# Attention of two transformer layers: part of the softmax exponentials given to VectorE, and TensorE's order set by a list schedule

## The chip, the cores and the metric

One core of one Trainium2 chip. The time is the device time of one execution in microseconds (us), the median over several executions. A kernel's profile is one execution with every instruction recorded. In its lines PE is TensorE, PEld its weight loads, DVE VectorE, ACT ScalarE, POOL GpSimd.

## The reference, cut to what matters

```
x = x + attention(layernorm(x))      # S=2048, D=640, 32 heads of 20
x = x + mixer(layernorm(x))          # 2048 -> 1536 -> 2048 over the tokens, gelu
(both once more, same weights)

scores = einsum("bhqd,bhkd->bhqk", q, k) * 20 ** -0.5
p = softmax(scores)                  # 32 x 2048 x 2048 exponentials a layer
o = einsum("bhqk,bhkd->bhqd", p, v)
```

A head has 20 values, padded to 32. The kernel works in *units* of 4 heads x 128 keys x 512 queries: 512 units, or 2048 single-head pieces ("heads" below, each 128x512), a layer. A *group* is the 16 units that share 4 heads and 512 queries; there are 32 groups a layer.

## The kernel before

Scores come from 64-row matmuls with half of the query rows masked, two at a time, and are repeated where TensorE has nothing else to do. One ScalarE instruction takes three heads:

```python
def s_matmul(St, slot, n, j):
    qb, g, kt = units[n]; jj = j // 2
    q = qm_tiles[(qb, g)][j % 2]                      # masked copy of Q
    pe(nc.tensor.matmul(St[:, slot, :], lhsT=KT[64 * jj:64 * jj + 64, g, kt * 128:(kt + 1) * 128],
                        rhs=q[64 * jj:64 * jj + 64, :], start=True, stop=True, tile_position=(64 * jj, 0)))
def emit_exp(t):
    nc.scalar.activation(out=P[:, 0:ncs, :]..., in_=St[:, 0:ncs, :]..., func=ACT.Exp, scale=SCALE)
# loop over tiles: scores of t+1 (repeated if no side work is at hand), exp of t,
# products P x V of older units, then a budget of side work (projections, output product,
# a partial mixer product per query block)
```

Each row block is layer-normed twice before the mixer. The products of a group add up in one PSUM tile `acc`, which VectorE transposes and normalizes.

The softmax here doesn't subtract the row's maximum and nothing guards it: scores larger than these inputs give would overflow.

## Time and profile before

| | us |
|---|---|
| time, median of 12 runs (2116.21 to 2120.33) | 2117.78 |
| span of the profiled run | 2114.6 |
| attention 1, first to last exponential | 923.8 |
| attention 2 | 924.2 |
| all else | 266.7 |

The attention rows are the distance from the start of the first exponential to the end of the last in the timeline (48.9 to 972.7 and 1098.2 to 2022.3).

### The profile page before, as it was taken

How to read it: one execution, taken by the hardware profiler on the slowest of the kernel's cores; microseconds unless marked ns; L12 is line 12 of the kernel's file. 1: busy time of each engine (PE TensorE's matmuls, PEld its weight loads, DVE VectorE, ACT ScalarE, POOL GpSimd, SP SyncE). 2: the span in 40 equal slices, each digit the busy share in tenths (PEclk: the TensorE clock that was granted, in tenths of full speed). 3: DMA queues.
4: the chain of work that ended last, by engine and by line, in shares of the span. 5: the costliest groups of instructions: out<-in, count | busy, mean ns of one | idle time of the engine just before them, and what ended most of it. 6: DMA issues, size and time to landing. Idle time of an engine off the chain costs nothing.

```text
span 2114.6 us, 31885 instructions
## 1 busy us (share of the span) xinstructions
PE 1924.5 (91%) x13100; PEld 655.4 (31%) x13278; DVE 623.9 (30%) x1391; ACT 1934.8 (91%) x1508; POOL 166.8 (8%) x250
## 2 busy tenths in 40 slices
PE   7999999999999999896999999999999999999969
PEld 4222222233223323222542222222332233232235
DVE  6122233212422042223542122332123221422252
ACT  5999999999999999995449999999999999999952
POOL 2000000110012001100000000001000110111000
PEclk9999999999999999998999999999999999999989
DMA  5000000110034012223620000101100430232145
GB/s 129 1 1 1 1 20 19 61 53 10 29 63 65 1 38 43 37 42 94 213 81 1 1 1 1 35 25 61 45 26 26 75 53 1 57 50 39 33 120 181
DMA packets 90739, 96.89 MB, mean 46 GB/s; under 512 B 9696, under 2 KB 68192, under 8 KB 90592
## 3 DMA queue, kind: packets, MB, share of 16 engines
q1 hardware_dynamic: 70464, 71.22, 10.9%
q0 software_dynamic: 20128, 23.62, 7.6%
q8 instruction: 104, 1.70, 0.4%
q14 instruction: 43, 0.35, 0.1%
HBM read 55.48 MB, written 39.32 MB: 45 GB/s over the span
## 4 chain that ended last, share of the span: by engine, by line
ACT 58%; PE 24%; issue 13%; DVE 4%; DMA 1%; POOL 1%; SPq 0%; another core or an unknown queue 0%; POOLq 0%; ACTq 0%; DVEq 0%
ACT P L345 57%; PE S L317 10%; PE y L746 4%; PE acc L551 3%; PE misc L223 3%; PE pp L214 1%; DMA ua<-uacc 1%; PE misc L453 1%; DVE bnst L158 1%; POOL rstd L165 1%; DVE bnst L159 0%; DVE utmp L685 0%; PE pp L223 0%; DVE T L354 0%; DMA x0in<-in_A_x_dram 0%
## 5 line engine op out<-in xcount | busy, mean ns | idle before, releaser
L345 ACT ACTIVATE P<-S 128x1536 bf16<-128x1536 f32 (+1 forms) x1366 | 1839.7, 1502 | 9.7 <-PE S L317 9.0
L317 PE MATMUL S<-qev,KT 64*128 64x512 bf16 x2962 | 836.2, 377 | 102.1 <-ACT P L345 95.5
L317 PE MATMUL S<-qod,KT 64*128 64x512 bf16 x3052 | 837.9, 379 | 20.8 <-ACT P L345 3.7
L317 PEld LDWEIGHTS <-KT 64*128 64x128 bf16 x6014 | 326.3, 93 | 657.1 <-issue 487.8
L551 PE MATMUL acc<-P,Vaug 128*32 128x512 bf16 x4096 | 409.9, 389 | 6.2 <-DVE T L354 4.3
L551 PEld LDWEIGHTS <-Vaug 128*32 128x32 bf16 x4096 | 106.5, 92 | 439.0 <-issue 439.0
L432 DVE COPY ustg<-misc 128x512 f32<-128x512 f32 (+1 forms) x144 | 70.1, 487 | 291.8 <-PE misc L426 261.1
L165 POOL TENSOR_TENSOR rstd<-veps,mhalf 128x1 f32<-128x1 f32 x96 | 54.0, 563 | 1194.3 <-DVE veps L163 1167.3
L437 POOL DMA_DIRECT2D uacc<-ustg x96 | 83.0, 864 | 464.8 <-DVE ustg L432 434.9
L746 PE MATMUL y<-uT,w2s 128*128 128x128 bf16 (+1 forms) x754 | 106.7, 297 | 4.2 <-ACT uT L689 2.7
L426 PE MATMUL misc<-h2st,w1st 128*128 128x128 bf16 (+1 forms) x524 | 105.0, 295 | 5.0 <-issue 2.9
L513 DVE CAST QTq<-misc 128x512 bf16<-128x512 f32 x62 | 42.9, 691 | 205.5 <-PE misc L223 205.5
L513 DVE CAST KT<-misc 128x512 bf16<-128x512 f32 x56 | 38.7, 691 | 212.0 <-PE misc L223 207.7
L354 DVE STREAM_TRANSPOSE T<-acc 128x512 f32<-128x512 f32 x64 | 45.9, 717 | 182.8 <-PE acc L551 182.8
L223 PE MATMUL misc<-hh,wq_pad 128*128 128x512 bf16 x272 | 91.0, 386 | 0.1
L276 DVE TENSOR_SCALAR qev<-QTq,mask_ev 128x512 bf16<-128x512 bf16 x64 | 22.5, 352 | 228.7 <-PE S L317 228.2
L223 PE MATMUL misc<-hh,wk_pad 128*128 128x512 bf16 x254 | 82.1, 385 | 1.5 <-issue 1.3
L746 PEld LDWEIGHTS <-w2s 128*128 128x128 bf16 x768 | 59.6, 98 | 50.0 <-issue 5.3
L453 PE MATMUL misc<-wo_pad,attnT 128*128 128x128 bf16 (+1 forms) x361 | 71.8, 298 | 0.6 <-issue 0.6
L76 ACT CAST Vaug<-pp 128x500 bf16<-128x500 f32 (+1 forms) x32 | 14.3, 454 | 50.5 <-PE pp L214 50.5
L426 PEld LDWEIGHTS <-w1st 128*128 128x128 bf16 x576 | 33.9, 97 | 61.1 <-issue 58.8
L462 DVE TENSOR_TENSOR x1s<-misc,xin 128x512 f32<-128x512 f32 (+1 forms) x48 | 23.5, 490 | 98.1 <-PE misc L453 98.1
(81 smaller groups left out, 788.7 us busy)
## 6 DMA issues: line engine op xcount, KB each, us to landing
uacc<-ustg POOLq DMA_DIRECT2D x72, 256.0 KB, 4.0
w2s<-in_B_w_dram SPq DMA_DIRECT2D x16, 768.0 KB
w1st<-in_B_w_dram SPq DMA_DIRECT2D x36, 256.0 KB
xd<-x1s SPq DMA_DIRECT2D x24, 320.0 KB
x1in<-xd SPq DMA_DIRECT2D x24, 320.0 KB
ua<-uacc SPq DMA_DIRECT2D x24, 320.0 KB
xd<-x2s SPq DMA_DIRECT2D x16, 320.0 KB
xin<-xd SPq DMA_DIRECT2D x16, 320.0 KB
```

Source lines behind the costliest of these rows:

```text
L165: nc.gpsimd.tensor_tensor(out=rstd[:], in0=veps[:], in1=mhalf[:], op=ALU.pow)
L223: pe(nc.tensor.matmul(t[:, :], lhsT=wpad[:, dt_, g, :], rhs=st.hT[:, dt_, tb * 512:(tb + 1) * 512], start=(dt_ == 0), stop=(dt_ == NDT - 1)))
L317: pe(nc.tensor.matmul(St[:, slot, :], lhsT=KT[64 * jj:64 * jj + 64, g, kt * 128:(kt + 1) * 128], rhs=q[64 * jj:64 * jj + 64, :], start=Tru ...
L345: nc.scalar.activation(out=P[:, 0:ncs, :].rearrange("p a b -> p (a b)"), in_=St[:, 0:ncs, :].rearrange("p a b -> p (a b)"), func=ACT.Exp, ...
L354: nc.vector.transpose(out=T1[:], in_=acc[:])
L426: pe(nc.tensor.matmul(t[:, 0:w], lhsT=states[fp]["w"][:, sti, ftl * 128:(ftl + 1) * 128], rhs=tiles4[sti][:, c0:c1], start=(sti == 0), sto ...
L432: nc.vector.tensor_copy(out=stg[:, 0:w], in_=t[:, 0:w])
L437: nc.gpsimd.dma_start(out=dst, in_=stg[:, 0:w], accum_op=ALU.add)
L453: pe(nc.tensor.matmul(t[:, 0:w], lhsT=attnT[:, g, ttl * 128:(ttl + 1) * 128], rhs=wo_pad[:, g, c0:c1], start=(g == 0), stop=(g == NG - 1)))
L513: nc.vector.tensor_copy(out=dst_ap, in_=t[:, :])
L551: pe(nc.tensor.matmul(acc[32 * j:32 * j + 32, :], lhsT=Vaug[:, (kt * H + hh) * VW:(kt * H + hh) * VW + 32], rhs=P[:, ci % 3, :], start=(kt ...
L746: pe(nc.tensor.matmul(y[:, 0:w], lhsT=w2s[:, ft, sl * 128:(sl + 1) * 128], rhs=uT[:, ft, c0:c1], start=(ft == 0), stop=(ft == NF - 1)))
```

## The change

Its intent: ScalarE's exponentials are the wall and VectorE is mostly idle, so VectorE takes some units. It turns a score into the bits of a bfloat16 power of two: J makes a fixed-point exponent in uint16, TT shifts and offsets it twice, and the sum of the two piecewise-linear results is close to a true exponential. Softmax divides by the sum of the weights, so a common factor doesn't matter. Core of the diff, with cuts marked by `...`:

```diff
-    R_DEFAULT=1, FILL_NOPV=3.0, ...
+SHIFTS = (0.0, 0.4927)
+NP_BUFS = 4; NJ_BUFS = 2; NT_BUFS = 5; ...
+# planned durations: PE_MM = 216.0, LAT_PE = 230.0, LAT_ACT = 240.0, LAT_V = 120.0 ...
-    lhsT=KT[64 * jj:64 * jj + 64, ...], rhs=q[64 * jj:64 * jj + 64, :]   # masked Q
+    lhsT=KT[32 * j:32 * j + 32, ...], rhs=get_QT(st, qb, g)[32 * j:32 * j + 32, :]
+            SLOT_N = (3, 2)                      # heads per ScalarE tile, in turn
+            def do_J(start):                     # one head, PSUM f32 -> uint16
+                nc.vector.tensor_scalar(out=d["jt"][:, j * 512:(j + 1) * 512], in0=Dt[:],
+                    scalar1=SCALE * LOG2E * 256.0, scalar2=127.0 * 256.0, op0=ALU.mult, op1=ALU.add)
+            def do_T(start):                     # four heads, one of two terms
+                nc.vector.tensor_scalar(out=tt_[:], in0=jt[:], scalar1=0.5, scalar2=TERM_C[i], ...)
+                ... tt_[...].bitcast(BF16)       # goes into the products like P
+            def warm(gap):                       # planned TensorE gap -> matmuls of zero weights
+                k = int(gap // PE_MM)
+                ...
+            # choice on TensorE: ScalarE's scores, VectorE's scores, products, side work
+            urgent = ("need" in f and is_urgent(f["need"])) or (gi >= NGR - 3 and not f.get("need"))
-            # in words: two layer norms per row block; partial mixer product per query block, added up by DMA
+            # in words: one layer norm (on GpSimd); one partial mixer product near the end, 12 row blocks deep
-                nc.vector.tensor_tensor(out=T2[:], ...)   # normalization
+                nc.gpsimd.tensor_tensor(out=T2[:], ...)
```

The kernel gives out PSUM in banks of 128x512 float32, eight in all: 3 + 2 for ScalarE's two tiles, one for VectorE's scores (SD), one for `acc`, one for side work.

## The prediction

> **What bounds the kernel now.** I read the page's busy shares and 40 slices first, then the chain that ended last.
>
> ```profile
> PE 1924.5 (91%) x13100; PEld 655.4 (31%) x13278; DVE 623.9 (30%) x1391; ACT 1934.8 (91%) x1508; POOL 166.8 (8%) x250
> ...
> ACT  5999999999999999995449999999999999999952
> ...
> ACT P L345 57%; PE S L317 10%; PE y L746 4%; PE acc L551 3%; PE misc L223 3%; PE pp L214 1%; DMA ua<-uacc 1%; PE misc L453 1%; DVE bnst L158 1%; POOL rstd L165 1%; DVE bnst L159 0%; DVE utmp L685 0%; PE pp L223 0%; DVE T L354 0%; DMA x0in<-
> ```
>
> Two engines look full, but there are two plateaus of ACT at 9 with a dip between (the first mixer) and a drop at the end (the second), and the exponential holds the chain. Next, the costliest groups tell which of the two is really full.
>
> ```profile
> L345 ACT ACTIVATE P<-S 128x1536 bf16<-128x1536 f32 (+1 forms) x1366 | 1839.7, 1502 | 9.7 <-PE S L317 9.0
> L317 PE MATMUL S<-qev,KT 64*128 64x512 bf16 x2962 | 836.2, 377 | 102.1 <-ACT P L345 95.5
> L317 PE MATMUL S<-qod,KT 64*128 64x512 bf16 x3052 | 837.9, 379 | 20.8 <-ACT P L345 3.7
> ```
>
> ScalarE lost only 9.7 us ahead of 1839.7 us of exponentials, while TensorE waits for ScalarE. There are 6014 score matmuls in the records where two layers need 2 x 2048 = 4096: a third are the deliberate repeats of the code, so TensorE's 91% is padded. ScalarE is the wall and VectorE, at 30%, is the engine with room. Then I cut the span by stage (start; attention 1; mixer 1; attention 2; mixer 2).
>
> ```profile
> core 0: us, PE busy (x) PEld busy (x) DVE busy (x) ACT busy (x) POOL busy (x), PEclk, DMA share, GB/s
> 0.00:46.60 46.60, 33.42 (x258) 20.51 (x263) 34.40 (x120) 25.82 (x49) 12.71 (x26) 1.00 0.62 139
> 46.60:966.50 919.90, 852.86 (x5767) 265.45 (x5842) 236.16 (x486) 914.28 (x681) 67.69 (x96) 1.00 0.13 28
> 966.50:1096.50 130.00, 109.17 (x790) 62.07 (x802) 74.95 (x205) 47.85 (x63) 13.71 (x24) 0.92 0.49 156
> 1096.50:2016.00 919.50, 852.11 (x5762) 265.14 (x5837) 236.12 (x486) 914.22 (x680) 67.71 (x96) 1.00 0.14 31
> 2016.00:2114.60 98.60, 76.94 (x528) 42.24 (x537) 42.23 (x96) 32.58 (x39) 4.96 (x8) 0.91 0.53 161
> ```
>
> So each attention is 920 us, nearly all of it ScalarE, and the rest is 46.6 + 130.0 + 98.6 = 275 us.
>
> **What the Trainium skill says.**
> - "VectorE: DVE Perf Modes", section "The perf-mode tier table": a tensor_scalar between 16-bit SBUF tensors runs at four elements a cycle, 693 ns for 2048 elements; with a PSUM operand it falls to at most two, and to one for float32 (section "Why PSUM operands drop a tier"). The trace agrees in kind: 128x512 bf16 through tensor_scalar took 352 ns, under the 533 ns of one element a cycle at that page's 0.96 GHz; a cast of 128x512 from PSUM took 691 ns.
> - "TensorEngine Tiling (Array Packing)", section "Key Properties": a change of tiling mode drains TensorE. The trace agrees: matmuls of one mode start 0.21 us apart, but a value product that follows a score matmul starts 0.30 us after it, and a full-array one 0.34 us after the products. A switch costs about 0.1 us.
> - "TensorE: Matmul & The Clock Gate", section "Measured speedup vs the span model": four 32-row matmuls together gain 3.07 times. Not in this trace, which has two 64-row tiles; its four 32-column products do share 0.40 us.
> - "SBUF — State Buffer", section "SBUF: two separate sides": a VectorE instruction in a two-port mode and a GpSimd one exclude each other. No number for it in this trace.
>
> **The change part by part** (per layer, 512 units of 4 heads x 128 keys x 512 queries).
> 1. *It moves some units' exponential to VectorE.* Per unit: 4 instructions J, one head each, PSUM 128x512 to uint16, and 2 instructions TT on 2048 uint16, whose bits are read as bf16 and both multiplied into the accumulator. J is a 128x512 read of PSUM: 691 ns, less the overlap with its neighbour. Two VectorE instructions of 692 and 280 ns lasted 0.89 us together in the first tail, so the overlap is 82 ns; J costs 609 ns. TT: 693 (the skill's; no record before) less 82 is 611 ns. A unit is 4 x 609 + 2 x 611 = 3.66 us of VectorE.
> 2. *ScalarE's tiles become 3 and 2 heads in turn.* Before: 1839.7/1366 = 1347 ns for 3 heads. The record lasts 1503, so neighbours overlap by 156; the few 128x1024 records last 1089, hence 933 each. Five heads take 2280 ns, 456 a head, 1.82 us a unit (against 1.80).
> 3. *VectorE's other work.* 236 us per attention now. Out go the two query masks (32 x 0.70 = 22), the multiply of the normalization, now on GpSimd (32 x 0.69 = 22), the second layer norm (12 tiles: from about 3.9 to 1.2 us, 32) and two thirds of the partial sums' evictions (36 x 0.97 down to 12 x 0.97, 23). Left: 236 - 99 = 137 us.
> 4. *Ideal split.* With x units on VectorE: 1.82(512 - x) = 3.66x + 137, so x = 145 and both end at 668 us. That needs both engines without a gap.
> 5. *Why not ideal.* VectorE's scores have one PSUM bank. J (0.69), then a matmul and its latency (0.42 us from the start of a matmul to the eviction in the trace) make 1.14 us per head before any queueing at TensorE; with 0.2 for queueing and delays by other VectorE work, four heads take about 5.5 us, in whose gaps the two TT and the other work fit. x = 720/5.5 = 131. VectorE is then 131 x 3.66 + 137 = 616 us busy, and ScalarE 381 x 1.82 = 693 us; at about 96% occupied (the two-head tile leaves little time to refill the other bank set) this is 720 us.
> 6. *TensorE.* At 0.213 us: 610 score tiles, 130 us; say 60% of 524 single VectorE heads not hidden beside another, 67; products (381 + 2 x 131) x 4/4, 137, and a fifth more for incomplete quartets, 164; projections 59 x 5, 63; output projection and first mixer product, about 80. Sum 504 us. At 0.1 us a switch and about 4.5 switches per five heads (305 periods) come 137 us: 641 of 720, 89%. It fits, but barely; TensorE's repeats are gone.
> 7. *Tail.* One layer norm instead of two saves about 5 us after each attention; the GpSimd multiply and small instructions give back about 2. Net 3 each.
>
> Sum: 275 + 2 x 720 - 2 x 3 = 1709 us span. The time was 4.5 us above the span before (2119.1 against 2114.6), so **1714 us**.
>
> **The rivals.**
> - *TensorE takes over.* For: step 6 has 89% and a static order cannot refill a missed slot; a full-array filler of two matmuls plus a switch is 0.53 us, while the slack for the three-head tile is 933 less about 0.7 us. Against: the repeats were a third of the score matmuls and 4 row tiles overlap. It gives attentions near 775 us, 1825 us in all, and ScalarE would wait for S.
> - *TT is not at four elements a cycle* (unsigned integers, or the shared port). At two, TT is about 1.15 us, a unit 4.74 us; the ideal is 709, realistically 760, 1795 us in all. Against: dtype width and placement are what the page names.
> - *The single bank's loop is slower*, 6.3 us per unit: x = 118, ScalarE 717 us of work, about 745 us an attention, 1765 in all.
> - *The schedule is nearly perfect*, 680 us: 1635. For: the order comes from a list schedule whose durations (67 + 426.7 per head, 216, 600, 610) match the trace.
> - *The new tail costs more*: the last block's weights are loaded only after the partial mixer product ended. If that ends in the tail, some 10 us per layer are exposed. Its priority is raised in the last three groups, so I doubt it.
>
> **Range and chances.** Attention from 680 to 770 us gives 1634 to 1814; I take 1630 to 1810. The work moved is far larger than any of these terms: even the TensorE rival is 14% faster. Faster by over 2%: 0.97; within 2%: 0.015; slower: 0.015, for a throttled clock or a badly broken order.
>
> **What would show it.** Attention windows of 700 to 740 us with ScalarE 95 to 97% busy and about 1520 heads there per layer, VectorE 80 to 88%; J near 690 and TT near 690 ns; about 130 units a layer on VectorE (4 J and 2 TT each); a granted clock still 1.00 in attention. Wrong if ScalarE's idle ahead of its exponentials passes 8% with S as releaser (TensorE rival), if TT is over 1 us, or if VectorE's units are under 120. The start and the mixers should keep their 275 us within 10.

## More of the kernel before

The prediction shows the page's busy shares, chain and groups. One more line of the chain of waits, shares of the span by engine, is needed for comparison later:

```profile
ACT 58%; PE 24%; issue 13%; DVE 4%; DMA 1%; POOL 1%; SPq 0%; another core or an unknown queue 0%; POOLq 0%; ACTq 0%; DVEq 0%
```

ScalarE holds most of the chain; TensorE holds a quarter, and about half of that is its scores and products in attention (10% and 3% in the list by line, which the prediction shows).

## The result, and the profile after

| | before | after |
|---|---|---|
| time, median | 2117.78 (12 runs) | 1762.33 (8 runs, 1758.67 to 1770.1) |
| attention 1 / 2, first to last exponential | 923.8 / 924.2 | 748.5 / 754.1 |
| all else | 266.7 | 258.0 |
| heads a layer on ScalarE / VectorE | 2048 / 0 | 1556 / 492 |

The ratio is 0.8325 (95% interval 0.8311 to 0.8338). A ratio here is the mean time of one kernel's fast runs over that of the other's in the same rounds, so it isn't quite the ratio of the medians.

The page of the changed kernel, busy shares and the chain of waits by engine:

```profile
PE 1658.2 (94%) x12645; PEld 552.3 (31%) x12804; DVE 1341.2 (76%) x2348; ACT 1524.9 (87%) x1388; POOL 178.8 (10%) x298
...
PE 62%; DVE 17%; ACT 12%; issue 6%; DMA 1%; POOL 1%; SPq 0%; ACTq 0%; DVEq 0%; POOLq 0%
```

VectorE went from 30% to 76%. The chain has moved: 58% on ScalarE before, 62% on TensorE now. Shares of a chain are no proof where three engines wait on one another, but this is a first hint that TensorE has little slack left.

The groups of instructions, by shape (count, then busy us and mean ns, then idle time before them with its releasers):

```profile
L850 ACT ACTIVATE P<-S 128x1536 bf16<-128x1536 f32 x622 | 913.2, 1468 | 56.9 <-PE acc L479 38.9 <-PE S L351 9.1 <-PE SD L351 3.0
L802 DVE TENSOR_SCALAR J<-SD 128x512 uint16<-128x512 f32 x984 | 671.1, 682 | 254.2 <-PE SD L351 248.9 <-PE S L351 3.6
L850 ACT ACTIVATE P<-S 128x1024 bf16<-128x1024 f32 x622 | 648.6, 1043 | 17.1 <-PE acc L479 15.4 <-PE S L351 1.2
L823 DVE TENSOR_SCALAR TT<-J 128x2048 uint16<-128x2048 uint16 x492 | 343.3, 709 | 7.7
```

The 984 J are four per unit in two layers: 123 units a layer. ScalarE lost 74 us in all, VectorE waited 249 us for its scores from TensorE.

The span cut by stage (start, attention 1, mixer 1, attention 2, mixer 2), as in the prediction:

```profile
core 0: us, PE busy (x) PEld busy (x) DVE busy (x) ACT busy (x) POOL busy (x), PEclk, DMA share, GB/s
0.00:48.00 48.00, 35.00 (x261) 20.99 (x266) 34.26 (x111) 26.08 (x50) 12.72 (x26) 1.00 0.58 124
48.00:797.60 749.60, 718.98 (x5556) 214.12 (x5622) 601.88 (x996) 715.00 (x624) 72.39 (x110) 1.00 0.09 25
797.60:918.00 120.40, 107.01 (x769) 61.79 (x780) 67.73 (x176) 42.09 (x59) 15.06 (x34) 0.94 0.56 184
918.00:1673.00 755.00, 724.24 (x5555) 214.08 (x5622) 601.96 (x996) 715.44 (x624) 72.35 (x110) 0.99 0.09 27
1673.00:1760.60 87.60, 73.00 (x507) 41.36 (x514) 35.38 (x69) 26.31 (x33) 6.29 (x18) 0.94 0.68 214
```

ScalarE is busy 95% of attention 1, VectorE 80%. But attention isn't even. Three stretches of it, in the same columns:

```profile
150.00:250.00 100.00, 96.20 (x730) 27.73 (x741) 82.46 (x131) 98.67 (x86) 4.19 (x4) 1.00 0.00 1
...
650.00:715.00 65.00, 62.48 (x501) 18.64 (x508) 53.42 (x93) 63.40 (x57) 3.94 (x5) 1.00 0.13 35
715.00:797.60 82.60, 78.24 (x625) 28.25 (x634) 58.39 (x98) 62.47 (x55) 7.53 (x12) 1.00 0.29 81
```

On the plateau ScalarE is 98 to 99% busy. In the last 83 us it is 76% busy and loses 20 us. The timeline there, in order of start (start, duration, engine, line, operation, count, idle time before):

```profile
714.79 4.75 ACT L850 ACTIVATE P<-S 128x1536 bf16<-128x1536 f32 x4
...
719.85 0.60 PE L724 MATMUL misc<-hh,w1st 128*128 128x512 bf16 x2
720.39 0.39 PE L351 MATMUL S<-QT,KT 32*128 32x512 bf16 x2
...
720.71 1.04 PE L724 MATMUL misc<-hh,w1st 128*128 128x512 bf16 x4
721.68 0.39 PE L351 MATMUL SD<-QT,KT 32*128 32x512 bf16 x1
...
721.99 0.40 PE L479 MATMUL acc<-TT,Vaug 128*32 128x512 bf16 x4
722.22 0.81 PE L479 MATMUL acc<-P,Vaug 128*32 128x512 bf16 x10
...
722.71 7.00 ACT L850 ACTIVATE P<-S 128x1536 bf16<-128x1536 f32 x6 [3.18 <-PE acc L479]
```

This is the urgent branch of the diff at work. In the last three groups matmuls of the mixer product (L724) go ahead of the products. The products are what empties ScalarE's four P buffers. Scores are ready, but ScalarE has nowhere to write: it stands still for 3.18 us until a batch of ten products is let through. The mixer product could start at 662 us, and only 62 of its matmuls were recorded before 715, against 206 in the 83 us that follow.

### The profile page after: what moved, and what is told of

Same layout as the page of the kernel before. It is cut to its first block, busy times and chain, and to the rows that moved or that the text cites.

```text
span 1760.6 us, 31505 instructions
## 1 busy us (share of the span) xinstructions
PE 1658.2 (94%) x12645; PEld 552.3 (31%) x12804; DVE 1341.2 (76%) x2348; ACT 1524.9 (87%) x1388; POOL 178.8 (10%) x298
## 4 chain that ended last, share of the span: by engine, by line
PE 62%; DVE 17%; ACT 12%; issue 6%; DMA 1%; POOL 1%; SPq 0%; ACTq 0%; DVEq 0%; POOLq 0%
PE acc L479 16%; PE S L351 15%; ACT P L850 12%; PE SD L351 8%; DVE J L802 7%; PE misc L248 6%; PE y L1123 6%; DVE TT L823 4%; PE misc L635 3%; PE misc L724 3%; PE pp L239 2%; DVE T L498 2%; PE acc L968 1%; PE acc L965 1%; DMA ua<-uacc 1%
## 5 line engine op out<-in xcount | busy, mean ns | idle before, releaser
L850 ACT ACTIVATE P<-S 128x1536 bf16<-128x1536 f32 (+1 forms) x1246 | 1429.6, 1254 | 74.0 <-PE acc L479 54.3
L802 DVE TENSOR_SCALAR J<-SD 128x512 uint16<-128x512 f32 x984 | 671.1, 682 | 254.2 <-PE SD L351 248.9
L351 PE MATMUL S<-QT,KT 32*128 32x512 bf16 x3112 | 494.4, 384 | 17.9 <-ACT P L850 7.2
L351 PE MATMUL SD<-QT,KT 32*128 32x512 bf16 x984 | 371.6, 378 | 15.4 <-DVE J L802 10.4
L823 DVE TENSOR_SCALAR TT<-J 128x2048 uint16<-128x2048 uint16 x492 | 343.3, 709 | 7.7
L351 PEld LDWEIGHTS <-KT 32*128 32x128 bf16 x4096 | 169.0, 91 | 495.9 <-issue 479.2
L479 PE MATMUL acc<-TT,Vaug 128*32 128x512 bf16 x1968 | 277.6, 387 | 9.4 <-DVE T L498 5.0
L724 PE MATMUL misc<-hh,w1st 128*128 128x512 bf16 (+1 forms) x524 | 93.9, 301 | 3.6 <-issue 1.9
L965 PE MATMUL acc<-wq_pad,zw 32*128 32x512 bf16 x232 | 80.1, 378 | 0.0
L968 PE MATMUL acc<-wq_pad,zw 128*32 128x512 bf16 x210 | 75.5, 383 | 0.0
L724 PEld LDWEIGHTS <-w1st 128*128 128x128 bf16 x576 | 37.2, 97 | 50.9 <-issue 38.0
```

Source lines behind the costliest of these rows:

```text
L351: pe(nc.tensor.matmul(dst, lhsT=KT[32 * j:32 * j + 32, g, kt * 128:(kt + 1) * 128], rhs=get_QT(st, qb, g)[32 * j:32 * j + 32, :], start=Tr ...
L479: pe(nc.tensor.matmul(acc["tile"][32 * j:32 * j + 32, :], lhsT=Vaug[:, (kt * H + hh_) * VW:(kt * H + hh_) * VW + 32], rhs=ap, start=(acc[" ...
L724: pe(nc.tensor.matmul(t[:, 0:c1 - c0], lhsT=w1t[ft][:, sti, :], rhs=h2_view[:, sti, c0:c1], start=(sti == 0), stop=(sti == NS - 1)))
L802: nc.vector.tensor_scalar(out=d["jt"][:, j * 512:(j + 1) * 512], in0=Dt[:], scalar1=SCALE * LOG2E * 256.0, scalar2=127.0 * 256.0, op0=ALU. ...
L823: nc.vector.tensor_scalar(out=tt_[:], in0=jt[:], scalar1=0.5, scalar2=TERM_C[i], op0=ALU.mult, op1=ALU.add)
L850: nc.scalar.activation(out=P[:, 0:n, :].rearrange("p a b -> p (a b)"), in_=St[:, 0:n, :].rearrange("p a b -> p (a b)"), func=ACT.Exp, scal ...
```

## The experiments

**Theories.** *Loop theory* (the prediction's step 5): ScalarE is the wall, and what it keeps is set by VectorE's rate, which is set by the single score bank and the time until TensorE answers. *TensorE theory* (the first rival): TensorE's total work is the wall. *Occupancy theory*: VectorE's busy time is. A separate claim is that the last three groups lose their 20 us to the order, as just read. All runs below passed the comparison with the reference; that this test is coarse is shown by e3, which leaves most of a product out and passes too. Counts of units, fillers and left-over pieces are those of the built order. A filler (`warm` in the diff) is a matmul on zero weights that the order puts into a planned gap of TensorE.

**e1, no offload.** Is the gain the moved exponentials at all?

```diff
             def d_take():
-                if d["u"] is not None or not j_free:
-                    return
+                return
```

> The changed kernel with no unit ever given to VectorE; all else of the change stays (32-row score matmuls, tiles of 3 and 2 heads, single layer norm, late mixer product, list order). If the moved exponentials are the gain, ScalarE has all 2048 heads of a layer again: 2048 x 0.456 us / 0.985 is about 948 us an attention, so 2 x 948 + 256 for the other stages, about 2150 us, slightly slower than the kernel before. If the new order and the lighter side work carry a good part of the gain themselves, it lands under 2050 us.

2127.12 us in one run (state unknown, a single run), attentions of 930.2 and 942.4 us. All else of the change is worth nothing by itself: it came out 0.4% above the kernel before. What the change wins, it wins by sharing the exponentials. That the other parts make room for that is argued and not tested here.

**e2, one term.**

```diff
-SHIFTS = (0.0, 0.4927)
+SHIFTS = (0.0,)
```

> Only one of the two TT terms per unit (a coarser exponential on purpose, the result may be off). Per unit it takes 0.61 us of VectorE and 4 product matmuls of TensorE away. The built order still has only 125 units a layer on VectorE against 123. Loop theory (one score bank and TensorE's answer time set VectorE's rate; ScalarE is the wall): ScalarE's work falls by 0.5%, attention by 4 to 10 us, total 1740 to 1760. TensorE theory (its total work sets the time everywhere): 123 quartets at 0.213 us and their switches fewer, 26 to 40 us an attention, total 1680 to 1710. Occupancy theory (VectorE's busy time sets it): 123 x 0.61 = 75 us less of it, and the total under 1680.

1740.17 us (1729.04 to 1744.56), ratio to the kernel before 0.8198. That is the lower edge of the loop theory's range. A sixth of VectorE's work per unit is gone and so are 984 product matmuls, and time falls by 1.3% (1.5% by the ratios). VectorE's occupancy is out as the wall of the changed kernel. Between the other two theories e2 doesn't decide: the granted clock of the profiled run was 0.977, against 0.989, and the three runs fall from 1745 to 1729 us as their clock rises from 0.972 to 0.985. Continued to 0.989 that is about 1724 us (an estimate), between the two ranges.

**e3 and e4, the last three groups.** e3 cuts the mixer product inside attention to a twelfth; e4 keeps all of it but takes the urgency away.

```diff
 e3
-                        for sti in range(NS):
+                        for sti in range(1):
 e4
-  urgent = ("need" in f and is_urgent(f["need"])) or (gi >= NGR - 3 and not f.get("need"))
+  urgent = ("need" in f and is_urgent(f["need"]))
```

> The partial mixer product that runs inside attention does one matmul instead of 12 per tile (wrong result on purpose), with the same evictions and writes. If the last three groups lose their time to these matmuls, which go ahead of the products there, the ScalarE idle of about 20 us per layer in the last 83 us goes and so does the mixer work left for the tail: 18 to 22 us per layer, total about 1720. If the stretch is slow for another reason (reads of the weights, the end of VectorE's work, the clock), under 8 us per layer, total over 1745.

> The matmuls of the mixer product keep the low priority they have before the last three groups; nothing else changes. The order then reaches the end of attention with 10 pieces of the mixer product undone instead of 1. My theory: attention gets about 16 to 20 us shorter per layer, but the 10 pieces (about 15 us) and the load of the last weights behind them come back in the tail, so the total is within 1% of the changed kernel, 1745 to 1775. Rival: the undone pieces hide under the tail's own waits (about 13 us between the last exponential and the next matmul), and 25 us or more are won, under 1738.

e3: 1727.57 us (1724.75 to 1731.23), 35 us under the changed kernel, 17 a layer, just short of the 18 to 22 expected of the order. e4: 1761.68 us, the same as the changed kernel, and also as expected. Its attentions are 730.7 and 734.0 us, 18 and 20 shorter, and the work comes back behind them. From e4's timeline, the last exponentials and the first ScalarE instruction after them:

```profile
733.70 45.85 ACT L850 ACTIVATE P<-S 128x1536 bf16<-128x1536 f32 x40 [0.32 <-PE SD L351]
809.57 0.92 ACT L1009 ACTIVATE hh<-x1last,nmr,rt 128x640 bf16<-128x640 f32 x1 [30.03 <-POOL nmr L283]
```

ScalarE waits 30.03 us where the changed kernel waits 12.98. So the urgency costs what it saves: the mixer product needs about 17 us a layer that TensorE doesn't have to spare, and the order only decides in which stage they are paid.

**e5 and e6, a second score bank.** e5 is the control: ScalarE's tiles hold 2 + 2 heads, which frees a bank. e6 gives that bank to VectorE.

```diff
 e5
-            SLOT_N = (3, 2)
+            SLOT_N = (2, 2)
-NA_BUFS = 10
+NA_BUFS = 13
 e6, besides
-                Dt = psp.tile([128, 512], F32, name="SD")
+                b = d["nb"]; d["nb"] = 1 - b
+                Dt = psp.tile([128, 512], F32, name=f"SD{b}")
...              # at most two heads loaded; d["u"] is freed when the last head is issued
```

> Control for the next run: ScalarE's tiles hold 2 and 2 heads instead of 3 and 2, one score bank for VectorE as before, one PSUM bank left unused (the normalized tiles get 13 buffers instead of 10, which the next run needs). ScalarE pays 0.933 us for 2 heads, 0.467 a head against 0.456, and TensorE has a quarter more score tiles and switches. The built order has 126 units on VectorE. 386 x 4 x 0.467 = 721 us of ScalarE and shorter slack for each refill: attention 755 to 775, total 1790 to 1810 in both theories.

> As the run before, but VectorE's scores get the freed bank, so that TensorE can fill one while VectorE reads the other, and the next unit is begun as soon as the last head of one is issued. Loop theory: VectorE's wait for scores (250 us in the changed kernel) falls under 100, the order places 159 units a layer, ScalarE keeps 353 x 4 x 0.467 = 659 us, attention 695 to 725, total 1700 to 1740, faster than the control by 3% or more; some mixer pieces are left for the tail. TensorE theory: the extra units bring more scores and twice the products, TensorE is the wall already and the time is that of the control or worse, 1790 to 1830.

e5: 1805.81 us, as expected. e6: 1807.20 us (1790.15 to 1809.36): no gain over the control, so the loop theory missed its range by 67 us. First e5, then e6, the J and the exponential of each:

```profile
L852 ACT ACTIVATE P<-S 128x1024 bf16<-128x1024 f32 x1544 | 1443.2, 1047 | 109.0 <-PE acc L480 82.6 <-PE S L351 13.1 <-PE SD L351 7.9
L804 DVE TENSOR_SCALAR J<-SD 128x512 uint16<-128x512 f32 x1008 | 686.7, 681 | 261.1 <-PE SD L351 243.2 <-PE S L351 17.4
```

```profile
L853 ACT ACTIVATE P<-S 128x1024 bf16<-128x1024 f32 x1412 | 1336.3, 1032 | 168.6 <-PE acc L484 108.4 <-PE S L351 35.2 <-PE SD L351 19.3
L807 DVE TENSOR_SCALAR J<-SD 128x512 uint16<-128x512 f32 x1272 | 814.5, 678 | 52.6 <-PE SD L351 30.9 <-PE S L351 5.8 <-DVE TT L826 0.5
```

The mechanism did what it should: VectorE's wait for scores fell from 243 to 31 us and it took 159 units (1272 J / 8) instead of 126. But ScalarE, with less to do, now idles 169 us, mostly for products and scores of TensorE. That looks like TensorE as the wall, but two more lines of e6 say otherwise: its chain of waits by engine, and 150 to 250 us in the columns as above.

```profile
DVE 45%; PE 39%; ACT 7%; issue 5%; DMA 3%; POOL 0%; DVEq 0%; SPq 0%; ACTq 0%; POOLq 0%
```

```profile
150.00:250.00 100.00, 93.81 (x744) 27.91 (x756) 98.00 (x164) 90.73 (x97) 5.49 (x5) 1.00 0.01 1
```

With the second bank VectorE itself is full, 98% busy at full clock, and it holds more of the chain than TensorE. In the first 300 us of attention, at a clock of 1.00 (e5 0.99), e6 gets through 830 heads, its control through 804 and the changed kernel through 833 (counted from the records of J and the exponential). So the bank does win there. The gain is lost later, and the trace shows two places where it can have gone. The mean granted clock was 0.949 (0.73 from 350 to 450 us); e6's fast runs fall from 1809 to 1790 us as their clock rises from 0.948 to 0.968, and continued to the control's 0.985 that is about 1774 us (an estimate), 32 us under the control. And 11 pieces of the mixer product are left for the tail, none in e5: after the last exponential of attention 1 ScalarE waits 35.73 us, against 11.09. One reason for the lower clock may be that this order has gaps for only 76 fillers a layer, against 190 in e5 and 230 in the changed kernel.

**e7, VectorE's scores first.**

```diff
-  opts.append((max(st_(sd, "row"), d["bank_free"] + SD_WAIT), 1, 0, do_SD))
+  opts.append((max(st_(sd, "row"), d["bank_free"] + SD_WAIT), 0, WIN_S, do_SD))
```

> VectorE's score matmul gets the same top priority and look-ahead window as ScalarE's; nothing else changes. The built order has 132 units on VectorE against 123, and 7 mixer pieces are left for the tail. Loop theory: VectorE is answered sooner, ScalarE's work falls by 9 units, 16 us per layer, but ScalarE's own refills are delayed and the tail takes some mixer work: total 1735 to 1765. TensorE theory: no gain, 1760 or more.

1822.14 us, mean clock 0.958: the loop theory missed, and the TensorE theory's "1760 or more" holds, though it didn't say why it should be 60 us slower. VectorE got 132 units, and ScalarE's idle time before its exponentials doubled, from 74 to 152 us. The clock is not all of it: the two runs with the highest, 0.974, still took 1816 and 1817 us.

**e8, no filler.**

```diff
-                k = int(gap // PE_MM)
+                k = 0
```

> The filler matmuls on zeros in TensorE's planned gaps are left out; the order of all else is the same. If they only fill gaps, the time stays within 0.7% (1750 to 1775), with the granted clock still 1.00 in attention because real gaps are under 1 us. If they hold the clock up, the granted clock falls and the total passes 1780. If they are in the way of work that comes a little earlier than planned, it gets faster by over 0.7%.

1836.27 us (1816.32 to 1842.01), 74 us slower (68 by the ratios), with a mean clock of 0.91. Nothing but multiplications by zero were taken out. Two stretches of e8's attention 1, the columns as above (the clock stands before the last two numbers), and then its longest TensorE waits from 400 to 550 us:

```profile
150.00:250.00 100.00, 95.08 (x712) 27.31 (x720) 82.38 (x132) 98.69 (x87) 4.20 (x4) 1.00 0.00 1
...
450.00:550.00 100.00, 96.01 (x622) 23.97 (x626) 71.74 (x124) 87.84 (x77) 17.18 (x28) 0.80 0.09 29
```

```profile
PE S L351 <- ACT P L850: 1.3, 6, 0.3
...
PE SD L351 <- DVE J L802: 0.7, 3, 0.3
```

In the second stretch ScalarE falls to 88% busy, while the clock is at 0.80. The longest of TensorE's waits there lasted 0.3 us: the clock went down without any long gap.

**e9 to e12, on one chip (e8 in the table is from another): how the filler acts.** e9 is the changed kernel again; e10 also fills gaps of half a matmul; e11 fills only every second gap; e12 is e6 with the filling of e10.

```diff
 e10, e12
-                k = int(gap // PE_MM)
+                k = int((gap + 0.5 * PE_MM) // PE_MM)
 e11
+                n_gap[0] += 1 if k else 0
+                k = k if n_gap[0] % 2 else 0
```

> The changed kernel itself, on the chip of the next three runs, so that they can be compared under 1%. Expected 1758 to 1770 us, with the higher times at the lower mean granted clock, as in its eight runs before (1758.67 at 0.991, 1770.1 at 0.984).

> A filler matmul also goes into planned TensorE gaps from 108 ns on (469 fillers a layer against 230); the order of all else is the same. Clock theory (the fillers hold the granted clock): the dips go, mean granted clock 0.992 or more, spread of the runs under 5 us, median 0.2 to 0.5% below the changed kernel. Rival (fillers only delay real work, up to 0.1 us each for 239 of them): 0.3 to 1.5% slower.

> Every second filled gap is left empty (115 fillers a layer against 230). If the clock falls with the idle time bit by bit, this lies half way to the run without fillers: mean granted clock about 0.95, 1790 to 1815 us. If only stretches without any filler matter, 1760 to 1775.

> Two score banks for VectorE again, with fillers in gaps from 108 ns on (264 a layer against 76). If the lost clock (0.949) ate that run's gain, the mean granted clock comes back to 0.98 or more and the total falls to 1730 to 1765. If TensorE's capacity is the wall behind VectorE's wait, the clock comes back but the total stays at 1780 or more, as ScalarE then waits for the products of its tiles.

| run | filler a layer | mean clock, profiled run | median us | ratio to before |
|---|---|---|---|---|
| e8 | 0 | 0.910 | 1836.27 | 0.8644 |
| e11 | 115 | 0.959 | 1793.91 | 0.8466 |
| e9 (the changed kernel) | 230 | 0.993 | 1759.70 | 0.8307 |
| e10 | 469 | 0.993 | 1789.43 | 0.8443 |

Half the filler gives half of the loss: the mean of e8 and e9 is 1798. With more filler than the change has, the clock doesn't rise any further and the time goes up by 30 us (1.6%, just over the range of the rival in its expectation), which over twice 239 extra matmuls is 62 ns for each. That doesn't give TensorE's slack. The order counts 100 ns for a switch of tiling mode into a gap, and rebuilding it shows that 202 of the 239 extra fillers sit in such a gap; by its planned durations (216 ns a filler) they overrun their gaps by 34 us a layer, 143 ns each. So somewhat under half of what a filler delays TensorE reaches the end of the run.

e12: 1782.46 us (1780.52 to 1785.35) at a clock of 0.976. Against its control e5 the second bank is worth 1.1% (0.8413 over 0.8509), and it stays 1.3% behind the changed kernel (0.8413 over 0.8307), whose 3 + 2 heads it had to give up. The clock came back in part, ScalarE still idles 148 us before its exponentials (100 of it for products). The time is the TensorE theory's (1780 or more), if only just; its cause isn't shown by it. VectorE is as full as in e6 and holds 40% of e12's chain beside TensorE's 44%, the extra fillers delay work as in e10, and the 11 pieces are left for the tail again.

No run that computes the same thing beat the changed kernel. e2 is 1.3% faster, with a coarser exponential; whether that is good enough is a question of accuracy that the coarse comparison here does not settle.

## Why the prediction was right or wrong

The time lies in the stated range, 48 us above the point. By its parts:

- *Attention, step 5: 720 us predicted, 748.5 and 754.1 measured.* Two terms were mis-sized. The number of units on VectorE was 131 in the prediction and is 123. The eight units cost ScalarE 8 x 1.82 = 15 us a layer. VectorE's unit took longer than 5.5 us: from 48 to 715 us some 112 units were done (counted from its J and TT records, 1.5 a head), 5.9 us each, or 1.48 a head. For 431 J from 60 to 700 us the trace splits that into 0.68 of J, 0.19 until the next score matmul starts and 0.62 from there to the next J (all means). So TensorE's answer came within the 0.2 that I allowed; it is the last piece, 0.42 in the prediction and 0.46 at the median, that was too small, as VectorE is often still in another instruction when its score is there. The other term is the end of attention: 17 us a layer, as e3 and e4 show. 15 + 17 is 32; measured were 28.5 more in attention 1, since the plateau is better than the 96% that I took. Attention 2 lost another 6 us; its clock was 0.93 from 1420 to 1520 us.
- *The rival of the costly tail* named the right piece of work and drew the wrong conclusion. It said that the raised priority in the last three groups would prevent the damage. The raised priority is the damage, at the same price (e4: equal time with and without).
- *Step 6, TensorE fits at 89%*, is the step whose form was wrong. It added busy times and took the rest for slack. But TensorE's time isn't free: 62 ns were lost per added filler (e10), and 17 us a layer were won by taking most of the mixer product away (e3). The rival "TensorE takes over" put the attention near 775 us. It didn't come to that, because ScalarE is about 98% busy on the plateau. When VectorE is given more (e6, e7, e12), ScalarE waits more for TensorE (169, 152 and 148 us of idle time against 74), but the clock is lower too, and in e6 and e12 VectorE is full. Which of the three is the wall then is not shown.
- *"TensorE's repeats are gone"* overlooked what the diff puts in their place. The filler matmuls carry some 70 us (e8). The prediction gave a throttled clock 0.015 of its chances; the clock was held only because the change includes them.
- *ScalarE's tiles*: 456 ns a head predicted, 1429.6 us of its exponentials' busy time over 3112 heads is 459 measured. *J and TT*: 691 and 693 ns predicted, 682 and 709 (median 689) measured. *VectorE's busy time*: 616 predicted, 602 measured, in part by luck: J and TT were busy 443.2 us for those 112 units, 3.95 us a unit where 3.66 was predicted, which the eight missing units and lighter other work made up. *ScalarE's*: 693 predicted, 715 measured, from the eight units.
- *The other stages*: I took 275 - 6 = 269 us, and 258.0 were measured. My stage cuts had left about 8 us of exponentials in the 275, which were then counted twice (266.7 is the number by first and last exponential). The tail saved 4 us a layer where I had put 3. The time above the span was 1.7 us and not 4.5: I had set 2119.1 us of other runs against the span of a run that took 2116.32. These three are 14 us to the good.
- *Its signs*: ScalarE's 95% and VectorE's 80% of attention, J, TT and the clock came out as said. Two failed: attention of 700 to 740 us, and "275 us within 10" for the start and the mixers, which are 256.0 in the stage table.

Sum: 62.6 us too little in attention, 11 too much in the other stages, 2.8 too much above the span, 48.8 in all.

## What to carry to other kernels

When the wall is one engine's elementwise work and another engine is idle, sharing it pays, but look at the engine that feeds both: here nearly half of a delay on the feeder reached the end, and more work for the helper filled the helper, cost clock and won next to nothing. Compare such runs at their granted clocks before naming a wall. Late low-priority work that must be done before the end needs the feeder's time somewhere; raising its priority does not make it free, so count it in the sum. And do not take filler matmuls for waste before looking at the granted clock of a run without them.

## What the Trainium skill lacked or had wrong

- "TensorE: Matmul & The Clock Gate", section "Why this matters for your kernels", asks for no idle gaps over about 3 us to keep the clock. In e8 the granted clock fell to 0.80 for 100 us with no TensorE wait above 0.3 us in that stretch, and in one and the same order it fell with the filler left out (0.993, 0.959, 0.910). The page's section on a second failure mode does tell of a clock that swings through frequent short idle, but not how much idle that takes. These runs don't give the threshold either, and the number of fillers alone doesn't set the clock: the built order of e2 has 277 a layer at 0.977, that of e5 190 at 0.985.
- "TensorEngine Tiling (Array Packing)", section "Key Properties", says that a change of tiling mode drains TensorE, without a figure. The traces show about 0.1 us a switch (0.30 to 0.34 us between starts where 0.21 is usual), and with three modes in turn this fills what looks like slack.
- "VectorE: DVE Perf Modes", section "The perf-mode tier table", lists times for bf16 and float32 (its modes ask only for a 16-bit type). uint16 to uint16 reaches the same rate: median 689 ns for 2048 elements, against 693 for bf16 there. Float32 in PSUM to uint16 took 682 ns for 512.
- "SBUF — State Buffer", section "SBUF: two separate sides", states the exclusive lock between VectorE and GpSimd, by which the later of the two blocks, without a time for such a pair. In the changed kernel 20 of the 492 TT began 0.3 to 0.6 us into a GpSimd multiply and took 1.01 to 1.28 us instead of 0.69; each ended 0.55 us after the multiply. One of them in the timeline:

```profile
743.98 1.04 POOL L508 TENSOR_TENSOR T<-T,rden 128x512 bf16<-128x512 f32 x1 [2.45 <-DVE rden L504]
```

```profile
744.29 1.28 DVE L823 TENSOR_SCALAR TT<-J 128x2048 uint16<-128x2048 uint16 x1
```

The multiply ends at 745.02, and the TT 0.55 us later.
